# Attention and routing on one core: scores with the directions as weights, routing by groups of four, the current token's products on the vector and activation engines, four matmuls of zeros

## The chip, the core and the metric

The kernel runs on one core of a Trainium2 chip. The core has a tensor engine (PE, with its weight loads shown apart as PEld), a vector engine (DVE), an activation engine (ACT), a general engine (POOL) and a queue engine (SP) that issues most transfers. Each works through its own list of instructions in order and waits for the others by semaphores. The metric is the device time of one execution in microseconds (us); shorter is better.

## The reference, cut to what matters

Three stages follow each other: a linear attention with a decaying state, a mixture of experts that sends each token to the expert with the highest score, and a second mixture with a quota for each expert. The change touches the first stage and the routing for the second.

```
batch, n_heads, seq, head_dim = (4, 8, 768, 48)
for t in range(S):
    cur = np.einsum('bhd,bhe->bhde', u[None] * kt, vt)
    y[:, :, t] = np.einsum('bhd,bhde->bhe', rt, state + cur)
    state = wt[:, :, :, None] * state + np.einsum('bhd,bhe->bhde', kt, vt)
...
en = expert_emb / (np.linalg.norm(expert_emb, axis=-1, keepdims=True) + 1e-06)
logits = xn @ en.T / tau
expert_idx = np.argmax(logits, axis=1)
```

x has 3072 tokens of 384 numbers; there are 8 experts, so 8 directions (the rows of `en`).

## The kernel before, in words

The attention runs over 24 chunks, six of 128 tokens for each of the four batches. A chunk is called a step here. For each step the kernel does the following; lines are those of the kernel before.

- `s2`, on DVE: two scans make the products of decays, forward (`PI`, L283) and backward (`RI`, L291); with them r and k become `rp` (L289) and `kp` (L295). The current token's products are `z` = r times u (four ACT instructions, L298) times k (one POOL instruction on 128x512, L299).
- `s3`: PE turns `kp` into `pT` (ACT copies it to `kT`) and multiplies `kp` by `rp` (`A`, L317); DVE masks that to `am` (two instructions, L321). PE turns `z` (`pz`, L325), DVE sums it for each head to `cs` (L327), and POOL multiplies v by it to `cv` (L329).
- `s4`: PE makes the step's addition to the state (`KV`, L344) and the output `y` from the state before (`Sb`, L347) and from `am` (L350). DVE updates the state (`tm`, `Sc`), ACT copies it to `Sb` (L362), and DVE adds `cv` to `y`: that is `x` (L364), the 128 tokens that the next stage gets.
- `s5`, one step behind: PE turns `x` (`pX`, L375), ACT copies it to `xT` and takes the squares.
- `s6` and `s6b`, the routing: PE multiplies `xT` by the eight directions `enT` (L388); ACT copies the scores to `LG`; DVE finds the maximum, its index and the one-hot row `oh` (L391 to L397); three small matmuls (L398, L399, L401) count the tokens that went to each expert before; DVE picks the row's number from that and turns it into an integer, `di`.
- `s7`: POOL scatters the 128 rows of `x` to the list of their expert (`xg`, L421), two such transfers a step from step 9 on.

Beside this, from step 4 on, pieces of the first experts' weights are split in two parts: ACT rounds a piece to `whi` (L187), and POOL takes the rest, `wlo` (L188, twelve instructions on 128x768). `heat` (L263) puts matmuls of a block of zeros into PE's list, two behind `A` (`HA`) and five behind `y` (`HY`); nothing reads their result. The order on each engine is set by the framework's scheduler. Some of POOL's work (tables for a later stage, `wlo`, scatters) is held back until the next step's `cv` by `issue_after`.

Of the kernel before, what the change touches and what calls it, by code (L numbers as in the profile page):

```python
# [24 lines left out]
NST = B * NC  # L25
# [50 lines left out]
WNQ = 2  # L76
HA = 2
HY = 5
# [3 lines left out]
def tile_kernel(ctx: ExitStack, tc, rd, kd, wd, vd, ud, emb, tau, m1w1, m1w2, m1w2t, wg2, m2w1, m2w2, out):  # L82
# [41 lines left out]
    for t in seeds + Sb:  # L124
# [10 lines left out]
                            channel_multiplier=-1)  # L135

# [98 lines left out]
    with tc.tile_pool(name="ld", bufs=3) as ld, tc.tile_pool(name="wk", bufs=2) as wk, \  # L235
            tc.tile_pool(name="ps", bufs=1, space=PSUM) as ps:

        def route_consts():
# [12 lines left out]
            pE = ps.tile([128, KT, 128], F32, name="pX")  # L251
# [26 lines left out]
        def s2(st):  # L278
# [18 lines left out]
            for p in range(HP):  # L297
                nc.scalar.activation(z[:, p], rr[:, p], AF.Copy, scale=ut[:, p:p + 1])  # L298
            nc.gpsimd.tensor_tensor(z, z, kk, op=ALU.mult)  # L299
            d["PI"] = PI  # L300

        def s3(st):
# [26 lines left out]
            d["cvi"] = nc.gpsimd.tensor_tensor(cv, d["v"], bcast(cs[:, :, None], [128, H, D]), op=ALU.mult)  # L329
# [52 lines left out]
        def s6(st):  # L382
            d = G[st]
            xT = d["xT"]
            yn = G[st + 1]["y"] if st + 1 < NST else ps.tile([128, 512], F32, name="y", bufs=2)
            pG = d["pG"] = yn[:, DM:DM + 2 * E].rearrange("p (a e) -> p a e", a=2)
            for kt in range(KT):
                nc.tensor.matmul(pG[:, 0, :], xT[:, kt, :], enT[:, kt, :], start=(kt == 0), stop=(kt == KT - 1))  # L388
            nc.scalar.copy(LG[:, st, :], pG[:, 0, :])
            mx = wk.tile([128, 8], F32, name="mx")  # L390
            nc.vector.max(mx, LG[:, st, :])  # L391
            mi = wk.tile([128, 8], U32, name="mi")
            nc.vector.max_index(mi, mx, LG[:, st, :])
# [50 lines left out]
        for st in range(NST):  # L444
# [803 lines left out]
```

## Time and profile before

| | us |
|---|---|
| median of 3 runs (852.36 to 856.16) | 855.87 |
| the profiled execution's own time | 852.17 |
| its span, first to last instruction | 850.4 |
| step 0's `x` begins | 24.0 |
| step 23's `x` begins | 225.9 |
| first transposition of the second stage's rows | 243.2 |

The span lies 1.8 us inside the execution's time. The attention takes the first quarter of it; after 243 us the two mixtures follow, which the change leaves as they are.

### The profile page before, as it was taken

How to read it: one execution, taken by the hardware profiler on the slowest of the kernel's cores; microseconds unless marked ns; L12 is line 12 of the kernel's file. 1: busy time of each engine (PE TensorE's matmuls, PEld its weight loads, DVE VectorE, ACT ScalarE, POOL GpSimd, SP SyncE). 2: the span in 40 equal slices, each digit the busy share in tenths (PEclk: the TensorE clock that was granted, in tenths of full speed). 3: DMA queues.
4: the chain of work that ended last, by engine and by line, in shares of the span. 5: the costliest groups of instructions: out<-in, count | busy, mean ns of one | idle time of the engine just before them, and what ended most of it. 6: DMA issues, size and time to landing. Idle time of an engine off the chain costs nothing.

```text
span 850.4 us, 14966 instructions
## 1 busy us (share of the span) xinstructions
PE 776.8 (91%) x5484; PEld 681.1 (80%) x5484; DVE 554.7 (65%) x1740; ACT 319.9 (38%) x763; POOL 227.9 (27%) x220
## 2 busy tenths in 40 slices
PE   5898998999989998999989999697979889899997
PEld 3787787888659897998989787485868778789997
DVE  9688899999534355344543546676878778787430
ACT  3334444443323454344443411423323323235431
POOL 4235477853200303203123002302021210112011
PEclk9799899999989999999999999787969979899999
DMA  8567457661253243433523002422323242426300
GB/s 277 167 193 247 137 185 249 189 202 39 66 181 116 102 149 100 158 114 106 184 88 105 5 1 84 150 87 100 124 72 140 80 154 94 145 69 223 122 29 29
DMA packets 39303, 107.66 MB, mean 127 GB/s; under 512 B 6666, under 2 KB 16700, under 8 KB 39228
## 3 DMA queue, kind: packets, MB, share of 16 engines
q1 hardware_dynamic: 32060, 87.71, 31.5%
q0 software_dynamic: 7168, 18.98, 6.3%
q8 instruction: 44, 0.72, 0.3%
q14 instruction: 31, 0.25, 0.1%
HBM read 87.16 MB, written 19.90 MB: 126 GB/s over the span
## 4 chain that ended last, share of the span: by engine, by line
PE 46%; issue 15%; DVE 4%; POOL 2%; DMA 1%; ACT 1%; another core or an unknown queue 1%; ACTq 0%; POOLq 0%; DVEq 0%
PE pY L520 7%; PE pY L518 7%; PE pY L519 6%; PE pH L518 6%; PE pH L519 6%; PE pH L520 6%; PE pO L657 2%; PE pcm L1081 1%; PE pcn L953 1%; DVE wlo L1120 1%; PE pX L624 1%; POOL x L1094 1%; POOL out_dram L1163 1%; PE pX L1134 1%
## 5 line engine op out<-in xcount | busy, mean ns | idle before, releaser
L515 DVE SCALAR_TENSOR_TENSOR hl<-pH,hh 128x416 fp32r<-128x416 f32 x64 | 37.6, 589 | 66.4 <-ACT hh L514 48.5
L518 PE MATMUL pH<-xhi,whi 128*128 128x416 f32 x192 | 72.1, 376 | 9.5 <-DVE hl L515 7.8
L1120 DVE TENSOR_TENSOR wlo<-stage,whi 128x384 fp32r<-128x384 f32 x128 | 68.3, 549 | 6.9 <-ACT whi L1119 6.8
L518 PE MATMUL pH<-x2h,whi 128*128 128x384 f32 x192 | 71.1, 371 | 1.8 <-DVE h2l L515 1.6
L734 POOL DMA_INDIRECT lg<-lr,ids x24 | 23.0, 959 | 179.6 <-DVE lr L659 173.2
L519 PE MATMUL pH<-x2l,whi 128*128 128x384 f32 x192 | 71.1, 371 | 0.0
L520 PE MATMUL pH<-x2h,wlo 128*128 128x384 f32 x192 | 70.1, 365 | 0.0
L1119 ACT CAST whi<-stage 128x384 fp32r<-128x384 f32 x128 | 57.0, 511 | 32.7 <-PE pH L519 19.3
L520 PE MATMUL pH<-xhi,wlo 128*128 128x416 f32 x192 | 69.0, 359 | 0.0
L519 PE MATMUL pH<-xlo,whi 128*128 128x416 f32 x192 | 68.6, 357 | 0.0
L518 PE MATMUL pY<-whi,h2h 128*128 128x384 f32 x192 | 67.7, 353 | 0.0
L520 PE MATMUL pY<-whi,h2l 128*128 128x384 f32 x192 | 67.7, 355 | 0.0
L1163 POOL DMA_INDIRECT out_dram<-orow,ix x24 | 24.3, 1015 | 159.3 <-ACT orow L1162 144.6
L519 PE MATMUL pY<-wlo,h2h 128*128 128x384 f32 x192 | 66.9, 350 | 0.0
L514 ACT ACTIVATE h2h<-pH 128x384 fp32r<-128x384 f32 x64 | 31.4, 490 | 93.8 <-PE pH L520 92.7
L188 DVE TENSOR_TENSOR wlo<-stage,whi 128x512 fp32r<-128x512 f32 x78 | 48.3, 684 | 24.8 <-ACT whi L187 24.8
L187 ACT CAST whi<-stage 128x512 fp32r<-128x512 f32 (+1 forms) x90 | 51.9, 647 | 31.5 <-PE pY L519 23.0
L520 PE MATMUL pY<-hh,wlo 128*128 128x416 f32 x168 | 60.5, 360 | 0.0
L518 PE MATMUL pY<-hh,whi 128*128 128x416 f32 x168 | 60.1, 359 | 0.0
L519 PE MATMUL pY<-hl,whi 128*128 128x416 f32 x168 | 59.1, 352 | 0.0
L350 PE MATMUL y<-vv,am 128*128 128x48 f32 x384 | 56.9, 273 | 0.0
L1094 POOL DMA_INDIRECT x<-y,ix x24 | 29.8, 1244 | 93.2 <-issue 52.4
(320 smaller groups left out, 1976.2 us busy)
## 6 DMA issues: line engine op xcount, KB each, us to landing
stage<-in_m1w_dram SPq DMA_DIRECT2D x32, 768.0 KB
stage<-in_m2w_dram SPq DMA_DIRECT2D x32, 768.0 KB
wz<-in_w_dram SPq DMA_DIRECT2D x24, 260.0 KB
rd<-in_r_dram SPq DMA_DIRECT2D x24, 256.0 KB
kd<-in_k_dram SPq DMA_DIRECT2D x24, 256.0 KB
xg<-zt SPq DMA_DIRECT2D x8, 627.2 KB
xr<-xg SPq DMA_DIRECT2D x24, 193.0 KB
vv<-in_v_dram SPq DMA_DIRECT2D x24, 192.0 KB
```

Of the source, the lines that this page charges most:

```text
L187: nc.scalar.copy(hi[:, s], t[:, o:o + g])
L188: (eng or nc.vector).tensor_tensor(lo[:, s], t[:, o:o + g], hi[:, s].bitcast(F32), op=ALU.subtract)
L350: yi = nc.tensor.matmul(y[:, o:o + D], ams[h][:, p, :], vv[:, 2 * p + h, :], start=(c == 0), stop=(c == 0 or h == 1))
L514: nc.scalar.activation(hi, pH, AF.Relu)
L515: nc.vector.scalar_tensor_tensor(lo, pH, 0.0, hi.bitcast(F32), op0=ALU.max, op1=ALU.subtract)
L518: nc.tensor.matmul(o, wh, xh, start=start, stop=False)
L519: nc.tensor.matmul(o, wh, xl, start=False, stop=False)
L520: pe[0] = nc.tensor.matmul(o, wl, xh, start=False, stop=stop)
L1094: gi = nc.gpsimd.indirect_dma_start(out=xr[:, a, :], out_offset=None, in_=y1, in_offset=bass.IndirectOffsetOnAxis(ap=ix[:, a:a + 1], axis=0))
L1119: nc.scalar.copy(hi[:, c], t[:, r * g:r * g + g])
L1120: (nc.vector if e == "v" else nc.gpsimd).tensor_tensor(lo[:, c], t[:, r * g:r * g + g], hi[:, c].bitcast(F32), op=ALU.subtract)
L1163: s_ = nc.gpsimd.indirect_dma_start(out=out, out_offset=bass.IndirectOffsetOnAxis(ap=d["ix"][:, a:a + 1], axis=0), in_=orow, in_offset=None)
```

## The change

The scores of a step become a product with the directions as the stationary operand: 8 rows by 128 tokens, written to partitions 32i to 32i+7 of the last quarter of one PSUM tile, `pxl`, whose first three quarters take `pX`. After four steps (the groups are 4, 4, 4, 4, 4, 2, 1, 1) `choose` copies that quarter, turns it once on PE and does the choice for all tokens of the group at once; `place`, a step later, does the counting matmuls for the group. `z` is four DVE instructions with two tensors and u in one. `cv` is eight ACT instructions, one a head. `HY` goes from 5 to 2, so a step has four matmuls of zeros. The `issue_after` is gone.

```
-HY = 5
+HY = 2
...
+        pxl = ps.tile([128, 512], F32, name="pX")
+        nc.vector.memset(pxl, 0.0)
...
             for p in range(HP):
-                nc.scalar.activation(z[:, p], rr[:, p], AF.Copy, scale=ut[:, p:p + 1])
-            nc.gpsimd.tensor_tensor(z, z, kk, op=ALU.mult)
+                nc.vector.scalar_tensor_tensor(z[:, p], rr[:, p], ut[:, p:p + 1], kk[:, p], op0=ALU.mult, op1=ALU.mult)
...
-            d["cvi"] = nc.gpsimd.tensor_tensor(cv, d["v"], bcast(cs[:, :, None], [128, H, D]), op=ALU.mult)
+            for h in range(H):
+                nc.scalar.activation(cv[:, h], d["v"][:, h], AF.Copy, scale=cs[:, h:h + 1])
...
+            i, n = slot_of[st]
+            lgt = pxl[32 * i:32 * i + E, DM:]
             for kt in range(KT):
-                nc.tensor.matmul(pG[:, 0, :], xT[:, kt, :], enT[:, kt, :], start=(kt == 0), stop=(kt == KT - 1))
...
-            nc.tensor.matmul(pG[:, 1, :], tri, oh, start=True, stop=False)
-            nc.tensor.matmul(pG[:, 1, :], ones, base8, start=False, stop=(cum[0] is None))
...
+                nc.tensor.matmul(lgt, enT[:, kt, :], xT[:, kt, :], start=(kt == 0), stop=(kt == KT - 1))
+
+
+        def choose(s0, n, y):
+            lt = wk.tile([128, 128], F32, name="lt", bufs=1)
+            nc.scalar.copy(lt, pxl[:, DM:])
+            nc.tensor.transpose(y[:, DM:], lt, ident)
+            lg = y[:, DM:].rearrange("p (i c) -> p i c", c=32)[:, :n, :E]
+            nc.scalar.copy(LG[:, s0:s0 + n, :], lg)
+            mx = wk.tile([128, GS], F32, name="mx")[:, :n]
+            nc.vector.reduce_max(mx, lg, axis=AX.X)
+            key = wk.tile([128, GS, E], BF16, name="key")[:, :n]
+            nc.vector.tensor_tensor(key, lg, bcast(mx[:, :, None], [128, n, E]), op=ALU.is_equal)
+            nc.vector.tensor_mul(key, key, rev4[:, :n])
+            km = wk.tile([128, GS], F32, name="km")[:, :n]
+            nc.vector.reduce_max(km, key, axis=AX.X)
+            oh = wk.tile([128, GS, E], BF16, name="oh")[:, :n]
+            nc.vector.tensor_tensor(oh, key, bcast(km[:, :, None], [128, n, E]), op=ALU.is_equal)
+            pre = wk.tile([128, GS + 1, E], BF16, name="pre")
+            nc.vector.tensor_copy(pre[:, 0], cum[0])
+            for i in range(n):
+                nc.vector.tensor_add(pre[:, i + 1], pre[:, i], oh[:, i])
+            cum[0] = pre[:, n]
+            return oh, pre[:, :n]
+
+        def place(s0, n, oh, pre, y):
+            pR = y[:, DM:DM + GS * E][:, :n * E]
+            flat = "p i e -> p (i e)"
+            nc.tensor.matmul(pR, tri, oh.rearrange(flat), start=True, stop=False)
+            nc.tensor.matmul(pR, ones, base4[:, :n].rearrange(flat), start=False, stop=False)
+            nc.tensor.matmul(pR, ones, pre.rearrange(flat), start=False, stop=True)
+            sel = wk.tile([128, GS, E], F32, name="sel")[:, :n]
+            nc.vector.tensor_mul(sel, pR.rearrange("p (i e) -> p i e", i=n), oh)
+            de = wk.tile([128, GS], F32, name="de")[:, :n]
+            nc.vector.reduce_sum(de, sel, axis=AX.X)
+            di = wk.tile([128, GS], I32, name="di", bufs=4)
+            nc.vector.tensor_copy(di[:, :n], de)
...
-            if st > 1:
-                s6b(st - 2)
             s4(st)
+            if chosen:
+                place(*chosen.pop(), G[st]["y"])
             if st > 0:
                 s6(st - 1)
-            with tc.issue_after(G[min(st + 1, NST - 1)]["cvi"].ins):
...
+            if st in ends:
+                chosen.append(ends[st] + choose(*ends[st], G[st]["y"]))
```

On DVE, this is the list from the backward scan of step 12 to the state of step 10, in the kernel before (`MAX` and `MAX_INDEX` are the search of the routing, `sel,de` the choice of the row's number):

```order
L291 SCALAR_TENSOR_TENSOR RI<-wz,seed_94 128x516
L395 CAST ef<-mi 128x1
L321 TENSOR_TENSOR am<-A,mask 128x512
L397 TENSOR_SCALAR oh<-io_102,ef 128x8
L295 TENSOR_TENSOR kp<-kd,RI 128x512
L406 TENSOR_TENSOR cum<-oh,cum 128x8
L327 TENSOR_REDUCE cs<-pz 128x8
L414 SCALAR_TENSOR_TENSOR sel,de<-y,oh 128x8
L357 TENSOR_TENSOR tm<-KV,Sc 128x192
L416 CAST di<-de 128x1
L364 TENSOR_TENSOR x<-y,cv 128x384
L359 TENSOR_TENSOR Sc<-tm,PI 128x192
```

The same place in the changed kernel, from the backward scan of step 6 to the state of step 4, ahead of the first choice:

```order
L303 SCALAR_TENSOR_TENSOR RI<-wz,seed_94 128x516
L310 SCALAR_TENSOR_TENSOR z<-rd,ut,kd 128x128
L307 TENSOR_TENSOR kp<-kd,RI 128x512
L310 SCALAR_TENSOR_TENSOR z<-rd,ut,kd 128x128 x2
L332 TENSOR_TENSOR am<-A,mask 128x512 x2
L338 TENSOR_REDUCE cs<-pz 128x8
L369 TENSOR_TENSOR tm<-KV,Sc 128x192
L376 TENSOR_TENSOR x<-y,cv 128x384
L371 TENSOR_TENSOR Sc<-tm,PI 128x192
```

Five of the routing's instructions are gone from between the large ones, three of the step's four `z` stand here instead, and both masks now stand together behind them.

On PE, the end of a step's `y` in the kernel before, with the counting matmuls between the last products (`tri` and `ones` are their weights):

```order
L347 MATMUL y<-Sb_96,rp 128x96
L350 MATMUL y<-vv,am 128x48
L398 LDWEIGHTS tri
L398 MATMUL y<-oh,tri 128x8
L399 LDWEIGHTS ones
L399 MATMUL y<-base_108,ones 128x8
L401 LDWEIGHTS ones
L401 MATMUL y<-cum,ones 128x8
L350 MATMUL y<-vv,am 128x48
L263 LDWEIGHTS ones
```

The same place in the changed kernel:

```order
L359 MATMUL y<-Sb_96,rp 128x96
L362 MATMUL y<-vv,am 128x48 x2
L275 LDWEIGHTS ones
L275 MATMUL KV<-hz,ones 128x320
L275 LDWEIGHTS ones
L275 MATMUL KV<-hz,ones 128x320
L400 MATMUL pX<-xT,enT 8x128 x3
L320 MATMUL pT<-ident,kp 128x128 x4
L328 MATMUL A<-rp,kp 128x128 x8
```

No counting matmul stands inside `y` here, two matmuls of zeros follow it instead of five, and the scores moved from between the `A` products to ahead of them.

On ACT, one step of the kernel before:

```order
L311 COPY kT<-pT 128x512
L365 COPY x<-idf 128x2
L379 ACTIVATE sqb,ss<-x 128x384
L362 COPY Sb_96<-Sc 64x4x48 x2
L389 COPY LG<-y 128x8
L298 ACTIVATE z<-rd,ut 128x128 x2
L377 COPY xT<-pX 128x384
```

One step of the changed kernel:

```order
L322 COPY kT<-pT 128x512
L341 ACTIVATE cv<-vv,cs 128x48 x8
L374 COPY Sb_97<-Sc 64x4x48 x2
L389 COPY xT<-pX 128x384
L391 ACTIVATE sqb,ss<-x 128x384
L377 COPY x<-idf 128x2
```

The eight `cv` stand directly ahead of the copies of the state, which the next step's `y` waits for.

## Rows read from the trace of the kernel before

**Rows 1.** Stretches: busy us by engine, granted clock, transfers' share, GB/s.
```profile
24.00:63.40 39.40, 36.36 (x327) 31.62 (x325) 30.88 (x80) 14.06 (x45) 11.30 (x13) 0.87 0.59 187
63.40:112.70 49.30, 44.42 (x392) 37.24 (x393) 43.14 (x100) 22.16 (x64) 25.05 (x21) 0.87 0.54 179
112.70:174.10 61.40, 56.42 (x557) 48.69 (x557) 60.88 (x139) 28.29 (x87) 47.51 (x35) 0.96 0.71 227
174.10:225.90 51.80, 51.09 (x509) 43.74 (x508) 43.72 (x125) 20.56 (x68) 20.84 (x19) 1.00 0.26 82
225.90:243.20 17.30, 12.81 (x56) 4.33 (x53) 7.41 (x54) 3.94 (x10) 2.91 (x7) 1.00 0.37 118
```

**Rows 2.** The same view, around places where the clock was lower.
```profile
31.60:41.80 10.20, 10.20 (x53) 8.68 (x52) 4.88 (x14) 2.42 (x8) 0.83 (x1) 0.50 0.50 159
69.40:79.40 10.00, 7.24 (x78) 5.75 (x77) 9.96 (x24) 3.05 (x10) 6.55 (x6) 1.00 0.67 232
79.40:82.80 3.40, 3.40 (x19) 2.58 (x20) 2.41 (x8) 0.54 (x2) 0.83 (x1) 0.51 0.46 140
```

**Rows 3.** Timeline, DVE, 197 to 234 us: start, us, instruction.
```profile
197.69 1.23 DVE L283 TENSOR_TENSOR_SCAN PI<-wz,ind 128x516 f32<-128x516 f32 x1
...
205.53 1.23 DVE L283 TENSOR_TENSOR_SCAN PI<-wz,ind 128x516 f32<-128x516 f32 x1
...
207.47 0.16 DVE L391 MAX8 mx<-LG 128x8 f32<-128x8 f32 x1
...
207.63 0.66 DVE L289 TENSOR_TENSOR rp<-rd,PI 128x512 f32<-128x512 f32 x1
...
210.13 0.22 DVE L397 TENSOR_SCALAR oh<-io,ef 128x8 bf16<-128x8 f32 x1
...
230.50 0.17 DVE L391 MAX8 mx<-LG 128x8 f32<-128x8 f32 x1 [1.01 <-ACT LG L389]
...
233.08 0.14 DVE L416 CAST di<-de 128x1 int32<-128x1 f32 x1
```

**Rows 4.** Timeline, POOL and DVE, 148 to 155 us.
```profile
148.12 2.01 POOL L188 TENSOR_TENSOR wlo<-stage,whi 128x768 fp32r<-128x768 f32 x1
148.49 2.73 DVE L283 TENSOR_TENSOR_SCAN PI<-wz,ind 128x516 f32<-128x516 f32 x1
...
153.39 1.49 POOL L299 TENSOR_TENSOR z<-z,kd 128x512 f32<-128x512 f32 x1
...
154.38 0.53 DVE L397 TENSOR_SCALAR oh<-io,ef 128x8 bf16<-128x8 f32 x1
```

**Rows 5.** Groups by line, 20 to 226 us: busy us, mean ns.
```profile
L283 DVE TENSOR_TENSOR_SCAN PI<-wz,ind 128x516 f32<-128x516 f32 x21 | 34.0, 1619 | 0.2
L299 POOL TENSOR_TENSOR z<-z,kd 128x512 f32<-128x512 f32 x22 | 32.9, 1496 | 42.2 <-ACT z L298 23.2 <-ACT x L365 16.7 <-DVE oh L397 2.1
...
L298 ACT ACTIVATE z<-rd,ut 128x128 f32<-128x128 f32 x84 | 28.6, 394 | 20.2 <-PE pz L325 8.8 <-issue 6.4 <-POOL wlo L188 4.9
...
L188 POOL TENSOR_TENSOR wlo<-stage,whi 128x768 fp32r<-128x768 f32 x12 | 24.8, 2070 | 9.3 <-ACT whi L187 9.3
...
L397 DVE TENSOR_SCALAR oh<-io,ef 128x8 bf16<-128x8 f32 x22 | 12.0, 548 | 0.1
...
L365 ACT COPY x<-idf 128x2 f32<-128x2 f32 x23 | 4.4, 190 | 0.1
```

**Rows 6.** Timeline, PE, 205 to 212 us.
```profile
205.38 0.81 PE L388 MATMUL y<-enT,xT 128*128 128x8 f32 x6
206.12 0.72 PE L317 MATMUL A<-rp,kp 64*128 64x128 f32 x8
206.77 0.45 PE L263 MATMUL KV<-hz,ones 128*128 128x320 bf16 x2
...
211.32 0.84 PE L263 MATMUL KV<-hz,ones 128*128 128x320 bf16 x5
```

**Rows 7.** Waits of PE, 20 to 226 us: total us, times, longest.
```profile
PE y L398 <- DVE oh L397: 10.0, 12, 1.6
```

More of the change, by code (lines that the diff above doesn't have):

```diff
@@ L76 @@
 WNQ = 2
+GROUPS = (4, 4, 4, 4, 4, 2, 1, 1)
+GS = max(GROUPS)
 HA = 2
-HY = 5
+HY = 2
 @with_exitstack
@@ new lines, in place @@
+        def place(s0, n, oh, pre, y):
[10 more added lines that the diff above has]
+            nc.vector.tensor_copy(di[:, :n], de)
+            for i in range(n):
+                ready.append((di[:, i:i + 1], G.pop(s0 + i)["x"]))
@@ L419, in s7 @@
         def s7():
             di, x = ready.pop(0)
-            s = nc.gpsimd.indirect_dma_start(out=xg, out_offset=bass.IndirectOffsetOnAxis(ap=di[:, :1], axis=0),
+            s = nc.gpsimd.indirect_dma_start(out=xg, out_offset=bass.IndirectOffsetOnAxis(ap=di, axis=0),
                                              in_=x, in_offset=None)
@@ L443, in tile_kernel @@
         early = (x for i, e in ((0, 0), (1, 0), (0, 1)) for x in wparts(i, e, WNQ, nc.gpsimd))
+        ends, chosen, slot_of = {}, [], {}
+        for n in GROUPS:
+            s0 = len(slot_of)
+            ends[s0 + n] = (s0, n)
+            for i in range(n):
+                slot_of[s0 + i] = (i, n)
         for st in range(NST):
@@ L457, in tile_kernel @@
                 s5(st - 1)
-            if st > 1:
-                s6b(st - 2)
             s4(st)
+            if chosen:
+                place(*chosen.pop(), G[st]["y"])
             if st > 0:
                 s6(st - 1)
-            with tc.issue_after(G[min(st + 1, NST - 1)]["cvi"].ins):
-                for _ in range(TB):
-                    if st > 1 and tables:
-                        table()
-                if st > WST:
-                    next(early, None)
-                if st == WF:
-                    wfold(E - DEF)
-                if st > E:
-                    for _ in range(NSC):
-                        if ready:
-                            s7()
+            if st in ends:
+                chosen.append(ends[st] + choose(*ends[st], G[st]["y"]))
+            for _ in range(TB):
+                if st > 1 and tables:
+                    table()
+            if st > WST:
+                next(early, None)
+            if st == WF:
+                wfold(E - DEF)
+            if st > E:
+                for _ in range(NSC):
+                    if ready:
+                        s7()
         for _ in early:
@@ L479, in tile_kernel @@
         s5(NST - 1)
-        s6b(NST - 2)
+        last_y = ps.tile([128, 512], F32, name="y", bufs=2)
+        place(*chosen.pop(), last_y)
         s6(NST - 1)
-        s6b(NST - 1)
+        end_y = ps.tile([128, 512], F32, name="y", bufs=2)
+        place(*ends[NST], *choose(*ends[NST], last_y), end_y)
         while ready:
```

42 lines of the change are left out of this document (10 added, 32 removed).

## The prediction

> **What bounds the kernel now.** I first cut the attention into stretches of whole steps [rows 1]; the reader is to see which engine is full in each. From 24.0 to 63.4 us (steps 0 to 4) PE works 36.36 of 39.40 us at a granted clock of 0.87. From 63.4 to 112.7 (five steps) PE and DVE both have gaps, 44.42 and 43.14 of 49.30, again at 0.87: a step takes 9.86 us. From 112.7 to 174.1 (seven steps of 8.77) DVE is full, 60.88 of 61.40. From 174.1 to 225.9 (seven steps, no `wlo` any more) PE is full, 51.09 of 51.80, at full clock; a step there takes 7.84 us from one forward scan to the next [rows 3]. So the bound changes hands, and what leaves one engine is worth little where the other is full.
>
> Next, what makes the two slow. DVE: the forward scan needs 1.23 us alone [rows 3], but 2.73 when it starts 0.37 us behind a `wlo` of 2.01 us on POOL; it ends 1.09 us after that one's end, as if it had started there [rows 4]. In the same way the small `oh` takes 0.53 beside POOL's `z` instead of 0.22 [rows 3, 4]. On average the scan takes 1.62 and `oh` 0.55 [rows 5]. PE: its longest sum of waits is for `oh`, 10.0 us in 12 waits, up to 1.6 us [rows 7]. Clock: from 31.6 to 41.8 us it stood at 0.50, the 1.2 GHz level, and from 79.4 to 82.8 at 0.51. In the 10 us ahead of the second fall PE worked only 7.24 us, while DVE was full [rows 2].
>
> **The change part by part.** *z on DVE.* Four instructions a step on 128x128. The trace has none of that form, so I go between two rows: 128x512 (`rp`) lasts 0.66, 128x8 (`mx`) 0.16, and starts lie 0.08 apart for two small ones (207.47 to 207.63 with one between), so about 0.08 of a duration is hidden [rows 3]. In a straight line from 0.08 at 8 to 0.58 at 512 elements, 128 cost 0.20 us; the ends are 0.15 (a quarter of 0.58) and 0.28 (nothing of the duration hidden). I take 0.20, nearest the small row: +0.8 us a step on DVE, 0.6 to 1.1.
>
> *Routing by groups.* Nine small DVE instructions a step go, at 0.08 each 0.72. A group has thirteen, on at most 32 elements; at 0.08 to 0.10 that is 1.2 for four steps, 0.3 a step. Net -0.4.
>
> *Relief from POOL.* `oh` loses its extra 0.33 us a step (0.548 against 0.22) [rows 3, 5]. POOL's 22 `z`, 32.9 us, go altogether, and `cv` with them; the twelve `wlo`, 24.8 us, stay, and keep their scans waiting [rows 5]. In sum DVE has +0.8 -0.4 -0.33: about nothing, +0.1 a step. The four `z` and the two full-width products are now the things that can run into `wlo`; that there is less to run into than before I count at nothing either way (end: 0.3 a step more, if each of the twelve `wlo` costs half a microsecond more).
>
> *PE.* Three matmuls of zeros fewer: (0.84 - 0.45)/3 = 0.13 each, 0.39 a step. The scores took 0.74 from their start to the next product's. They keep three products of two passes, now with 128 columns to move; the nearest row is `A` with 128 columns, 0.65 for eight, 0.081 a pass, so 0.49 (ends: 0.13 x 128/320 a pass, 0.3, and 0.74) [rows 6]. That is -0.25. Counting three times a group instead of a step, plus a transposition, is under -0.1. A full step falls from 7.84 to 7.15 us (6.9 to 7.4), and the waits for `oh` inside `y` disappear, because `place` comes a step later.
>
> The Trainium skill's price is lower: by TensorE: Matmul & The Clock Gate (LDWEIGHTS (loading the stationary operand), Back-to-back issue gap) a load scales with its columns, eight here, and 128 columns cost some 56 ns, so the scores would cost 0.33 and the step 7.0 (an estimate from that page); no row here shows such a load.
>
> *ACT.* Four `z` (0.394 each) go, eight `cv` come; between 0.19 (2 columns) and 0.394 (128 columns) 48 columns cost 0.26, so 2.1 for 1.6 [rows 5]. ACT is busy 28.29 of 61.40 [rows 1], so the sum is free. But the eight stand ahead of `Sb`, and wait for `cs` first. `tm`, `x` and `Sc` follow `cs` on DVE meanwhile, so `Sb` is later than before by what is left of the 2.1 us when `Sc` is done, at most about 1 us by my estimate. What is late next is the first product of the next `y` on PE. Its cover is the 1.5 us by which a step of 8.7 on DVE is longer than PE's 7.15. I count nothing; where PE sets the pace the cover is gone, and it costs up to 1 us a step.
>
> *Start and end.* Before 24 us DVE makes `z` for three steps (2.4 us) in a stretch where it also loses less to POOL: +1.5, between 0 and 2.4. At the end the last token's routing takes 230.50 to 233.08 and its rows leave then [rows 3]; now a 128x128 copy on ACT (0.394, as `z` [rows 5]) and a transposition with its hand-overs come ahead of it: +1.0 (0.4 to 1.5).
>
> **The sum.** Steps 0 to 4: 39.40 = four steps of 7.84, plus 5.1 lost to the half clock over 10.2 us, plus 2.9 of waiting; with 7.5 a step (PE 7.15 and hand-overs), the same clock and 1.4 less waiting, 36.5: -3. Steps 4 to 9: DVE's own 43.14 stays and the waits for `oh` go; PE needs 5 x 7.15 = 35.8 plus the clock's 0.13 x 49.3 = 6.4, so the end is near DVE's sum plus a few waits, 45: -4. Steps 9 to 16: DVE stays full: 61.4 to 60, -1.5, mostly since the `wlo` can now start without POOL's other work ahead of them and so lie earlier. Steps 16 to 23: the last two have no scans and are PE's, -0.6 each; the five before are DVE's at (43.72 - 6.8)/5 = 7.4 (I take 3.4 for each of the last two) against up to 7.84 now, -0.3 each: -2.5. Together -11, start and end +2.5: **-8.5 us**. From the profiled execution's own 852.2 that is 843.7, so **844**. The median of the runs is 3.7 us above that execution, so a median of the changed kernel could come out up to 847 with the same gain.
>
> **The rivals.** *DVE takes it all back (about no change).* If `z` costs 0.28, DVE gets 0.3 more a step, 6.3 us over the 21 steps whose scans lie behind 20 us [rows 5]; the gain shrinks to about 2 and the time is 850. For it: DVE full in 61 us of the attention. Against it: DVE's 128x8 rows at 0.16.
>
> *Slower: the clock falls more often.* DVE holds the pace, PE has 7.15 us of work in a step of 8.7 and three matmuls of zeros fewer, so the long stretch from step 9 on could go as steps 4 to 9 do now, at 0.87 and 9.86 us. That costs 7 x 1.1 = 7.6, from step 16 on 5 x 0.5 = 2.5 more, and steps 0 to 9 gain nothing; with start and end's 2.5 the time is about 865. For it: the fall behind 7.24 us of work in 10 [rows 2]. Against it: the single waits for `oh` are gone, and from 112.7 on PE worked 92% and the clock stood at 0.96. It decides from about seven falls of 3.4 us more than now, each worth half its length.
>
> *The clock stays up.* Then the 5.1 us of the first stretch and the 6.4 of the second come back too, as far as DVE lets them: -4 and -3 more, and 837. The row's fall came behind waits of 1.6 us at most [rows 2, 7], so shorter waits alone need not keep it up. The Trainium skill (TensorE: Matmul & The Clock Gate, HAM oscillation — how this bites in real kernels) has long idle gaps between bursts lower the clock; by that rule none is left here and this would be the result, but the rows do not bear it out.
>
> **How the numbers follow.** The forecast, 839 to 848: 0.52. No change: 0.20. Clock stays up, or DVE freed more than thought, 828 to 839: 0.15. Slower: 0.13. The range 834 to 858 leaves out about a third of the gain's far side and half of the slow side, some 2 in 10. The likeliest case alone has 839 to 848. A measurement of this kernel tells about 0.5% (4.3 us) from no change. Faster by more: the forecast and the clock case, with a little lost at the near end, 0.66; within: 0.21; slower by more: 0.13.
>
> **What would show it.** PE's step at the end near 7.2 us, waits of PE for `oh` gone, and in their place waits for `am` or `x` on DVE. DVE still over 95% from 112 to 165 us, with `z` near 0.28 as a duration and scans of 2.7 beside `wlo`. Scores near 0.5 us a step. The attention's last `x` near 216 instead of 225.9, and about 18 us from there to the second stage's first transposition. Wrong if `z` lasts over 0.35, if PE waits for `Sb`, or if rows of clock 0.5 appear after 113 us.

## The result, and the profile after

The changed kernel took 844.6 us in the median of 4 runs (840.2 to 846.3), the kernel before 855.6 beside it (852.4 to 856.2): a ratio of 0.989, with a 95% interval of 0.985 to 0.993. So it is faster by about 1.1%, and the forecast of 844 and its likeliest case came out. The profiled execution of the changed kernel, however, was the slowest of its four (846.3 us, span 844.4), and lies only 5.9 us below the profiled one of before. The traces below answer for those 5.9 us, the runs for 11. The medians and ranges given here are of all runs of a kernel; a run more than 1.5% above its kernel's fastest is left out of the ratios and of the differences between kernels.

The first view cuts the attention at the same steps as [rows 1]: 0 to 4, 4 to 9, 9 to 16, 16 to 23, and from the last `x` to the second stage. Columns: stretch and length, busy time of PE, PE's weight loads, DVE, ACT and POOL with the number of instructions, granted clock, DMA share, GB/s.

```profile
23.20:55.50 32.30, 30.59 (x306) 25.73 (x306) 31.97 (x62) 17.64 (x62) 3.82 (x2) 1.00 0.76 241
55.50:110.60 55.10, 46.93 (x361) 39.57 (x361) 49.95 (x95) 27.17 (x86) 22.99 (x13) 0.75 0.61 202
110.60:166.40 55.80, 53.95 (x519) 45.78 (x516) 53.25 (x122) 29.41 (x106) 10.26 (x9) 0.97 0.61 190
166.40:216.30 49.90, 49.43 (x473) 40.57 (x471) 42.92 (x117) 28.53 (x107) 8.10 (x8) 1.00 0.30 97
216.30:234.40 18.10, 12.50 (x57) 4.38 (x56) 8.02 (x56) 3.79 (x11) 4.86 (x9) 0.97 0.30 100
```

Against before the four stretches moved by -7.1, +5.8, -5.6 and -1.9 us, the tail by +0.8. So one stretch lost, and the others gained more than it. The second and the third belong together: DVE is busy 6.8 us more in steps 4 to 9 and 7.6 less in 9 to 16, since nine of the twelve pieces (a piece is one `whi` and its `wlo`) now lie in the first of the two and one in the second. In steps 4 to 9 DVE and PE have gaps besides (49.95 and 46.93 of 55.10), and the clock was granted at 0.75 where before it had 0.87.

Most of the first stretch's 7.1 us is clock: it held 1.00 here, and before it stood at 0.50 from 31.6 to 41.8 us [rows 2], which cost the 5.1 us that the prediction names. Just ahead of that fall PE had waited, until 29.81 us, for the directions to be made ready. It is the longest of PE's waits between 20 and 226 us in that trace, and the changed kernel's list, below, has none for them:

```profile
PE pX L253 <- DVE am L250: 2.3, 1, 2.3
```

But this gain is not steady. In another execution of the changed kernel (after_again, below) the clock fell at about 16 us, though PE had waited up to there no longer than here (6.3 and 2.1 us against 6.1 and 2.1, before the first products), and steps 0 to 4 took 39.7 us:

```profile
24.80:64.50 39.70, 39.70 (x304) 33.22 (x303) 29.14 (x62) 17.61 (x61) 2.15 (x2) 0.73 0.58 183
```

With the start (0.8 earlier) the attention and its tail give 8.8 us; the 610.0 us behind the second stage's first transposition were 607.2 before, which the change does not touch.

What happens in steps 4 to 9 is in the timeline around 68 us (start, duration, engine, line, operation; in brackets idle time and what ended it):

```profile
66.97 1.55 ACT L195 CAST whi<-stage 128x768 fp32r<-128x768 f32 x2
...
67.86 3.73 POOL L196 TENSOR_TENSOR wlo<-stage,whi 128x768 fp32r<-128x768 f32 x2 [14.38 <-ACT whi L195]
68.03 3.97 DVE L310 SCALAR_TENSOR_TENSOR z<-rd,ut,kd 128x128 f32<-128x128 f32 x3
...
71.92 1.28 DVE L332 TENSOR_TENSOR am<-A,mask 128x512 f32<-128x512 f32 x2
...
72.75 1.57 PE L328 MATMUL A<-rp,kp 64*128 64x128 f32 x9 [2.64 <-DVE am L332]
```

ACT casts two pieces in a row, POOL takes their `wlo` back to back, and three `z` on DVE, which alone need 0.33 each, last 3.97 together. `am` and the `A` behind it are late by that, PE stands for 2.64 us, and then the clock falls:

```profile
72.90:86.60 13.70, 13.70 (x77) 11.47 (x77) 9.90 (x21) 3.68 (x14) 4.54 (x4) 0.50 0.55 190
100.30:114.00 13.70, 9.46 (x49) 7.74 (x49) 11.75 (x24) 4.90 (x13) 5.88 (x3) 0.51 0.46 148
```

Before, the attention had one fall of 10.2 us and five of 3.4 ([rows 2] shows the first two), 27.2 us in all. Here there are one of 3.4, at 55.9 us, and these two of 13.7, together 30.8. The second begins amid seven `wlo` that POOL takes from 91.8 us on; a wait of PE of 4.24 us ahead of `A` lies inside it and so did not start it.

PE's sums of waits, to be held against [rows 7]:

```profile
PE A L328 <- DVE am L332: 4.4, 2, 2.6
PE A L328 <- DVE oh L417: 4.2, 1, 4.2
PE y L359 <- ACT Sb L374: 3.2, 3, 1.5
PE y L428 <- DVE oh L417: 1.0, 1, 1.0
```

The twelve waits for `oh` inside `y` have gone but for one. Two for `am` (2.64 and 1.71 us) took their place, with a third of 4.24 us (named `oh` ahead of `A`, it is the same kind: the list of DVE was late behind three `wlo`).

A step with no piece in it, on DVE, for [rows 3]:

```profile
181.57 0.55 DVE L376 TENSOR_TENSOR x<-y,cv 128x384 f32<-128x384 f32 x1
182.03 1.22 DVE L295 TENSOR_TENSOR_SCAN PI<-wz,ind 128x516 f32<-128x516 f32 x1
183.17 0.33 DVE L310 SCALAR_TENSOR_TENSOR z<-rd,ut,kd 128x128 f32<-128x128 f32 x1
...
186.07 0.61 DVE L310 SCALAR_TENSOR_TENSOR z<-rd,ut,kd 128x128 f32<-128x128 f32 x2
186.60 1.28 DVE L332 TENSOR_TENSOR am<-A,mask 128x512 f32<-128x512 f32 x2
...
188.52 0.55 DVE L376 TENSOR_TENSOR x<-y,cv 128x384 f32<-128x384 f32 x1
```

From `x` to `x` it takes 6.95 us, and no routing stands in it. (Taken from scan to scan, as 7.84 was before, the steps here take 7.26 to 7.49, in the mean 7.35.) Two `z` take 0.61, from start to the next start 0.53, so one costs 0.27.

PE in the same step, for [rows 6]:

```profile
186.70 0.43 PE L275 MATMUL KV<-hz,ones 128*128 128x320 bf16 x2
187.07 0.82 PE L400 MATMUL pX<-xT,enT 128*8 128x128 f32 x6
187.82 0.66 PE L320 MATMUL pT<-ident,kp 128*128 128x128 f32 x4
```

The scores take 0.75 to the next product's start, as before; the two matmuls of zeros 0.37.

The groups from 20 to 226 us, for [rows 5] (busy, mean ns, then idle time ahead):

```profile
L341 ACT ACTIVATE cv<-vv,cs 128x48 f32<-128x48 f32 x184 | 44.0, 322 | 22.7 <-DVE cs L338 22.1 <-DVE am L332 0.5
L310 DVE SCALAR_TENSOR_TENSOR z<-rd,ut,kd 128x128 f32<-128x128 f32 x86 | 38.8, 462 | 0.0
L295 DVE TENSOR_TENSOR_SCAN PI<-wz,ind 128x516 f32<-128x516 f32 x21 | 27.3, 1301 | 0.3 <-DVE sel L432 0.3
...
L196 POOL TENSOR_TENSOR wlo<-stage,whi 128x768 fp32r<-128x768 f32 x12 | 23.4, 1969 | 71.9 <-ACT whi L195 71.9
```

The scans lost most of their lengthening (1.30 for 1.62), and `z` took it over: 0.46 in the mean against 0.33 undisturbed. The Trainium skill (SBUF — State Buffer, Who interferes with whom) says that a VectorE operation with two inputs in SBUF and a GpSimd operation that reads SBUF shut each other out for a whole instruction. The trace agrees: `z` began 0.17 us behind the `wlo` and ended 0.4 us after the pair had.

### The profile page after: what moved, and what is told of

It reads as the page before. It is cut to its first block, busy times and chain, and to the rows that moved or that the text cites. A ratio compares the mean times of both kernels' runs of the same rounds, so it can differ in the third digit from the quotient of the medians.

```text
span 844.4 us, 14670 instructions
## 1 busy us (share of the span) xinstructions
PE 771.9 (91%) x5373; PEld 675.0 (80%) x5373; DVE 556.1 (66%) x1719; ACT 335.5 (40%) x851; POOL 168.0 (20%) x173
## 4 chain that ended last, share of the span: by engine, by line
PE 53%; issue 9%; DVE 4%; POOL 2%; another core or an unknown queue 1%; ACT 1%; DMA 1%; ACTq 0%; POOLq 0%; DVEq 0%
PE pH L548 8%; PE pY L550 7%; PE pY L548 7%; PE pH L549 7%; PE pH L550 7%; PE pY L549 7%; PE pO L687 2%; PE pX L654 2%; PE pcm L1111 1%; PE pcn L983 1%; DVE wlo L1150 1%; POOL x L1124 1%; POOL out_dram L1193 1%; PE pX L1164 1%
## 5 line engine op out<-in xcount | busy, mean ns | idle before, releaser
L548 PE MATMUL pH<-xhi,whi 128*128 128x416 f32 x192 | 73.8, 385 | 11.7 <-DVE hl L545 7.5
L544 ACT ACTIVATE h2h<-pH 128x384 fp32r<-128x384 f32 x64 | 31.4, 491 | 91.8 <-PE pH L550 90.8
L764 POOL DMA_INDIRECT lg<-lr,ids x24 | 23.1, 961 | 185.9 <-DVE lr L689 180.7
L544 ACT ACTIVATE hh<-pH 128x416 fp32r<-128x416 f32 x64 | 32.8, 515 | 62.5 <-PE pH L550 48.5
```

The costliest lines, as they stand in the source:

```text
L544: nc.scalar.activation(hi, pH, AF.Relu)
L548: nc.tensor.matmul(o, wh, xh, start=start, stop=False)
L764: s = nc.gpsimd.indirect_dma_start(out=dst, out_offset=bass.IndirectOffsetOnAxis(ap=d["ids"][:m, a:a + 1], axis=0), in_=src, in_offset=Non ...
```

## The experiments

Three sets ran, each on one chip, with the kernel before beside it. That kernel took 861.5, 838.4 and 859.8 us on the three, so kernels are compared within a set. The changed kernel itself ran in the second set alone. Two theories stood after the result. The first: the lists of DVE and PE became shorter, and steps 4 to 9 gave part of it back, since without `issue_after` the pieces come in bunches. The second: the clock falls because the matmuls of zeros are gone. That the new form of the scores saves PE's time was a third matter.

This table has the lengths of the stretches from `x` to `x` of each profiled execution, in us, with the granted clock of two of them; the rows that matter follow below. Each line is one execution, and the same kernel differs between executions: `changed` and `after_again` are one kernel, and so are `pace`, `pace_again` and `pace_base`.

| kernel (set) | steps 0-4 | 4-9 | 9-16 | 16-23 | sum | clock 0-4 | clock 4-9 |
|---|---|---|---|---|---|---|---|
| changed (result) | 32.3 | 55.1 | 55.8 | 49.9 | 193.1 | 1.00 | 0.75 |
| pace (1) | 29.1 | 45.6 | 63.7 | 51.9 | 190.3 | 1.00 | 1.00 |
| zeros5 (1) | 29.9 | 52.2 | 56.1 | 54.4 | 192.6 | 1.00 | 0.91 |
| tokens_as_weights (1) | 32.2 | 51.3 | 53.9 | 50.3 | 187.7 | 1.00 | 0.80 |
| after_again (2) | 39.7 | 51.5 | 55.7 | 49.9 | 196.8 | 0.73 | 0.92 |
| pace_again (2) | 29.0 | 45.7 | 62.0 | 49.8 | 186.5 | 1.00 | 0.96 |
| routing_by_step (2) | 35.4 | 54.7 | 57.0 | 52.4 | 199.5 | 1.00 | 0.78 |
| z_two_engines (2) | 30.0 | 42.4 | 63.5 | 50.0 | 185.9 | 1.00 | 0.96 |
| pace_base (3) | 29.1 | 45.6 | 62.1 | 50.4 | 187.2 | 1.00 | 1.00 |
| pace_vector (3) | 29.0 | 42.3 | 57.5 | 50.5 | 179.3 | 1.00 | 1.00 |
| pace_z (3) | 34.1 | 42.1 | 61.0 | 52.4 | 189.6 | 0.90 | 0.96 |
| pace_zeros5 (3) | 30.5 | 46.3 | 62.5 | 53.3 | 192.6 | 1.00 | 1.00 |

### The pieces spread over the steps

```
-                nc.scalar.activation(cv[:, h], d["v"][:, h], AF.Copy, scale=cs[:, h:h + 1])
+                d["cvi"] = nc.scalar.activation(cv[:, h], d["v"][:, h], AF.Copy, scale=cs[:, h:h + 1])
...
-                next(early, None)
+                with tc.issue_after(G[min(st + 1, NST - 1)]["cvi"].ins):
+                    next(early, None)
```

> The changed kernel, with one edit: the rounding of a weight piece on ACT is put behind the eight cv of its own step, so that one piece a step reaches POOL instead of two or three together. Theory one (bunched pieces): in steps 3 to 9 the gain is given back because POOL runs two or three wlo back to back, DVE's z waits for all of them, PE waits 1.7 to 4.2 us for am, and the clock falls to half for 30.8 us in all between 55 and 114 us. Then single pieces leave waits of at most 1.5 us, less than 14 us of half clock in the attention, and the time goes from 844.6 to 835 to 840. Theory two (zeros): the clock falls because three matmuls of zeros a step are gone; then spreading the pieces changes little, 843 to 846, with 25 us or more of half clock.

Measured: 843.5 us (842.2 to 853.4, 6 runs), a ratio of 0.984 (0.977 to 0.991) to before. The 835 to 840 that the first theory expected were missed (at this ratio 842 on the chip of the result); the half clock of the profiled attention was 13.7 us, in one fall, under the 14 of that theory, and its waits went up to 1.8 us where it had 1.5. Beside no run of the changed kernel the ratio could not be told from 0.989, so it was run again next to it:

> The pieces of weights spread over the steps again, beside the changed kernel on the same chip. The first theory (the bunches of pieces cost what steps 4 to 9 lost) expects 3 to 6 us under the changed kernel, since steps 4 to 9 took 55.1 us there and 45.6 us here in the earlier trace, less what steps 9 to 16 then pay for the pieces that came early (64 against 56 us). If a piece costs the same wherever it stands, the two are within 2 us. The second theory (the matmuls of zeros had held the clock) expects falls of the clock between 55 and 110 us here too.

> The changed kernel once more, as the measure for the three runs beside it on the same chip. Both theories expect a ratio of 0.985 to 0.992 to the kernel before and the same picture in the trace: wlo on GpSimd in bunches of two and three, two or three falls of the clock between 55 and 115 us.

Measured in that set: spread 823.7 (820.4 to 824.7, 5 runs), 0.982 (0.976 to 0.987); changed 829.3 (823.9 to 835.2, 11 runs), 0.990 (0.987 to 0.993). The spread pieces are 5.7 us faster in the medians; the intervals just touch. The clock granted over the whole execution was higher in each of the five runs with spread pieces (0.949 to 0.957) than in any of the eleven of the changed kernel (0.929 to 0.948). Where in the attention the 5.7 us lie, the two traces do not show: in steps 4 to 16 they take 107.2 us (changed) and 107.7, and their whole difference lies in steps 0 to 4, which the clock of after_again made long before the first piece. A third time (label pace_base) it was 844.0 us against 859.8 for before:

> The pieces spread over the steps, as the measure for the three runs beside it on the same chip: a ratio of 0.979 to 0.985 to the kernel before.

Its ratio of 0.986 (0.976 to 0.997) is a little above what was expected, within its interval. Its stretches:

```profile
23.60:52.70 29.10, 29.10 (x293) 24.51 (x291) 28.84 (x62) 15.42 (x58) 0.00 (x0) 1.00 0.73 239
52.70:98.30 45.60, 39.42 (x378) 33.33 (x377) 45.04 (x97) 24.60 (x83) 16.49 (x9) 1.00 0.77 240
98.30:160.40 62.10, 54.17 (x519) 45.54 (x518) 62.07 (x121) 33.59 (x113) 26.08 (x15) 1.00 0.54 173
160.40:210.80 50.40, 49.07 (x465) 40.13 (x461) 42.79 (x116) 28.10 (x106) 8.58 (x8) 1.00 0.33 108
```

With two matmuls of zeros behind `y` the clock stays at 1.00 through all 23 steps of this execution, and DVE is full from step 4 to 16. In the other two it fell once, for 13.7 us, and twice, for 3.4 each, and the clock of steps 4 to 9 was 1.00 and 0.96, where the changed kernel had 0.75 and 0.92. So few zeros alone do not take the clock away in this kernel; in these traces, and by the clocks of all runs of the second set, it falls more where the pieces lie in bunches. A single piece still costs what one of a bunch does, as the timeline at 83 us shows:

```profile
83.35 2.56 POOL L196 TENSOR_TENSOR wlo<-stage,whi 128x768 fp32r<-128x768 f32 x1 [5.57 <-ACT whi L195]
84.23 1.83 DVE L310 SCALAR_TENSOR_TENSOR z<-rd,ut,kd 128x128 f32<-128x128 f32 x1
85.98 0.68 DVE L307 TENSOR_TENSOR kp<-kd,RI 128x512 f32<-128x512 f32 x1
```

The `z` takes 1.75 us to the next start, 1.5 more than its 0.25 to 0.27 alone; in the bunch at 68 us it was 3.89 for three, 1.5 to 1.6 more for each of the two `wlo`. The DVE time lost to a piece is equal in these two places, so steps 9 to 16 are longer here (they now hold seven pieces instead of one) and steps 4 to 9 shorter. That what a bunch adds is PE's longer wait and the clock behind it fits the granted clocks, but it is argued: no single trace shows the 5.7 us.

### Five matmuls of zeros

```
-HY = 2
+HY = 5
```

> The changed kernel with five matmuls of zeros behind y instead of two. Theory one (bunched pieces): PE pays 0.39 us more in steps where it sets the pace, and the clock still falls in steps 3 to 9, over 20 us of half clock: 846 to 851. Theory two (zeros): the half clock between 55 and 114 us drops from 30.8 us to under 14 and the time to 836 to 842.

Measured: 849.5 us (845.3 to 863.6, 10 runs), 0.989 (0.985 to 0.993) to before: the same ratio as the changed kernel's. Each theory got one half right here. The half clock of the profiled attention fell to 13.6 us, under the 14 that the second theory asked for, and steps 4 to 9 have a clock of 0.91 for 0.75; but the 836 to 842 us that it expected did not come, and steps 16 to 23, where PE sets the pace, are 4.5 us longer than in the result's trace. In a kernel with bunches the zeros seem to give back about what they cost; the changed kernel did not run in this set, so that is read from the ratios alone. With the pieces spread it is another matter:

> As the spread pieces, with five matmuls of zeros a step instead of two. If PE sets the pace of the steps without a piece, 0.39 us a step comes back there (some eleven steps: 3 to 5 us more, up to 9 if every step pays). If the zeros lie in PE's waits and hold the clock, within 2 us, and no falls of the clock before 220 us.

Measured: 849.3 us (847.0 to 860.4, 10 runs) against 844.0 for pace_base beside it, 4.4 us more (ratios to before 0.991, 0.987 to 0.995, and 0.986, 0.976 to 0.997: by the intervals alone not told apart, but nine runs at 847.0 to 853.2 all lie above three at 843.3 to 844.0). The two profiled executions are 8.0 us apart, 5.4 of them between the sums of the stretches:

```profile
23.60:54.10 30.50, 30.50 (x306) 25.66 (x305) 28.98 (x61) 15.37 (x58) 0.00 (x0) 1.00 0.75 236
54.10:100.40 46.30, 42.25 (x400) 35.36 (x398) 44.94 (x96) 24.95 (x84) 15.74 (x9) 1.00 0.75 238
100.40:162.90 62.50, 59.99 (x540) 50.14 (x540) 59.37 (x120) 33.20 (x113) 23.64 (x15) 0.92 0.54 172
162.90:216.20 53.30, 51.21 (x484) 41.74 (x482) 43.26 (x117) 28.13 (x106) 8.58 (x8) 1.00 0.31 103
```

Of the 5.4, 1.4 are paid in steps 0 to 4 and 2.9 in 16 to 23, where no piece lies and PE is full; in the twelve steps between, which DVE paces, only 1.1. The clock gained nothing (0.92 in steps 9 to 16, and 0.941 to 0.953 over the nine whole executions, 0.939 to 0.952 over the three of pace_base). With the pieces spread the second theory is out.

The reverse, the kernel before with two instead of five:

```
-HY = 5
+HY = 2
```

> The kernel before with two matmuls of zeros behind y instead of five, alone. By theory one the zeros are only work: PE saves 0.39 us in the steps where it sets the pace (about eleven), -2 to -5 us, and the half clock of the attention stays near 24 to 27 us: 850 to 853. By theory two the clock falls more often: more than 35 us of half clock, 857 or more.

Measured: 856.0 us (848.3 to 870.2, 10 runs) against 861.5, a ratio of 0.992 (0.987 to 0.997), some 7 us. So alone, without the rest of the change, fewer zeros made the kernel before faster. But here the second theory had the clock right: the seven runs that the ratio counts were granted 0.908 to 0.927 over the whole execution, the kernel before beside them 0.925 to 0.942. Fewer zeros lowered the clock in that kernel, and it was faster in spite of it. The profiled execution took 864.0 us, and no row of it is read.

### The tokens as weights, as before

```
-            lgt = pxl[32 * i:32 * i + E, DM:]
+            lgt = pxl[:, DM + 32 * i:DM + 32 * i + E]
...
-                nc.tensor.matmul(lgt, enT[:, kt, :], xT[:, kt, :], start=(kt == 0), stop=(kt == KT - 1))
+                nc.tensor.matmul(lgt, xT[:, kt, :], enT[:, kt, :], start=(kt == 0), stop=(kt == KT - 1))
...
-            lt = wk.tile([128, 128], F32, name="lt", bufs=1)
-            nc.scalar.copy(lt, pxl[:, DM:])
-            nc.tensor.transpose(y[:, DM:], lt, ident)
-            lg = y[:, DM:].rearrange("p (i c) -> p i c", c=32)[:, :n, :E]
+            lg = pxl[:, DM:].rearrange("p (i c) -> p i c", c=32)[:, :n, :E]
```

> The changed kernel with the scores' operands put back: the tokens are the weights, and a step's scores lie at columns 32i to 32i+7 for all 128 tokens, so that the copy lt and its transposition go; the choice by groups stays. If the directions as weights cost PE the same (0.75 us for six passes in the changed kernel's trace, 0.74 before), the time stays or falls by up to 2 us, 842 to 845, most of it at the last token's routing (0.6 to 1 us). If they save PE 0.25 us a step, as I had put it, the time rises by 2 to 5 us, to 847 to 850.

Measured: 849.5 us (845.4 to 852.7, 4 runs), 0.989 (0.981 to 0.997). The scores in PE's timeline:

```profile
181.49 0.73 PE L400 MATMUL pX<-enT,xT 128*128 128x8 f32 x6
182.07 0.64 PE L320 MATMUL pT<-ident,kp 128*128 128x128 f32 x4
```

Six passes with eight columns to move and a full load each take 0.58 to the next start; the changed kernel's six, with eight columns to load and 128 to move, 0.75. The new form is the dearer one by 0.17 a step in this place. The old form took 0.74 in the kernel before, where products of `A` came next [rows 6], so its price hangs on its place in the list. The ratio is that of the changed kernel, as the first reading had it; that 849.5 lies in the range of the second is this chip, on which the kernel before took 861.5.

### Routing by step

```
-GROUPS = (4, 4, 4, 4, 4, 2, 1, 1)
+GROUPS = (1,) * 24
```

> Routing in groups of one step instead of four; all else as changed. If the lists on VectorE set the pace, about 0.4 us a step comes back (thirteen small instructions at 0.08 us a step instead of a quarter of them, less what four choices cost in one), and PE waits for the one-hot again where it stands behind a choice: 6 to 12 us more than the changed kernel. If the time of the routing was beside the path, 0 to 2 us.

Measured: 838.3 us (832.4 to 856.3, 11 runs), 0.999 (0.995 to 1.003) to before, and 8.4 us above the changed kernel beside it. All else of the change is in this kernel, and it is as slow as the kernel before. One step on DVE:

```profile
186.41 0.54 DVE L376 TENSOR_TENSOR x<-y,cv 128x384 f32<-128x384 f32 x1
...
190.81 0.16 DVE L412 TENSOR_TENSOR key<-y,mx 128x8 bf16<-128x8 f32 x1
190.88 0.34 DVE L310 SCALAR_TENSOR_TENSOR z<-rd,ut,kd 128x128 f32<-128x128 f32 x1
191.14 0.15 DVE L413 TENSOR_TENSOR key<-key,rev 128x8 bf16<-128x8 bf16 x1
191.22 0.34 DVE L310 SCALAR_TENSOR_TENSOR z<-rd,ut,kd 128x128 f32<-128x128 f32 x1
...
194.15 0.55 DVE L376 TENSOR_TENSOR x<-y,cv 128x384 f32<-128x384 f32 x1
```

Ten small instructions lie between the large ones, most 0.07 to 0.08 us from their start to the next; the step takes 7.74 from `x` to `x`, the changed kernel's step without routing 6.95. Three steps in a row from scan to scan, with the columns of [rows 1], in the kernel before, this one and the changed one:

```profile
181.64:205.53 23.89, 23.39 (x251) 20.55 (x247) 23.15 (x61) 10.88 (x37) 12.10 (x11) 1.00 0.31 91
171.80:195.70 23.90, 23.06 (x222) 18.98 (x220) 23.32 (x74) 13.13 (x51) 4.04 (x3) 1.00 0.43 129
174.77:196.81 22.04, 21.99 (x226) 18.59 (x226) 22.04 (x50) 11.90 (x43) 4.26 (x4) 1.00 0.32 101
```

By step, a step takes what it took before, 7.97 us; by groups it takes 7.35. DVE is busy 0.43 less a step and PE 0.36 less, because PE too turns the scores and counts in every step here. Both are nearly full, and which of the two savings was needed is not separated by a run. The waits of PE for `oh` are not back, since `place` still comes a step later: PE's largest sum of waits is 10.7 us in 8, for `am`. So the end of the waits that [rows 7] names did not by itself make this kernel faster than the one before.

### The current token's products on two engines

```
-                nc.vector.scalar_tensor_tensor(z[:, p], rr[:, p], ut[:, p:p + 1], kk[:, p], op0=ALU.mult, op1=ALU.mult)
+                nc.scalar.activation(z[:, p], rr[:, p], AF.Copy, scale=ut[:, p:p + 1])
+            nc.gpsimd.tensor_tensor(z, z, kk, op=ALU.mult)
```

> The products of the current token back on ScalarE (four activations) and GpSimd (one multiplication of 128x512); all else as changed. VectorE loses 1.07 us a step of z, but its scans meet GpSimd's multiplication again and take up to 2.7 instead of 1.2 us. The theory that VectorE's list paces the steps, and that the move was worth nothing by itself (1.07 paid, about 0.33 to 1.4 of slowed scans saved), expects within 4 us of the changed kernel, with no bunches of three pieces on GpSimd since its list is longer. If moving z off GpSimd was where the gain came from, 6 to 10 us more than the changed kernel.

Measured: 825.3 us (824.3 to 831.5, 5 runs), 0.988 (0.981 to 0.994), 4.0 below the changed kernel in the medians; by the intervals the two are not told apart. POOL's instructions now lie between the pieces, and most `wlo` stand alone or in pairs with a gap. With the pieces spread:

> As the spread pieces, with the products of the current token on ScalarE and GpSimd as before the change. With the pieces in bunches this was about 4 us less than the changed kernel. If that came from GpSimd's list (with z in it, the pieces could not stand back to back), nothing of it is left here: 0 to 8 us more than the spread pieces, as VectorE meets GpSimd's multiplication in every step. If moving z to VectorE was a loss in itself (1.07 us a step paid for 0.1 to 0.7 us of slowed scans), about 4 us less.

Measured: 846.4 (845.4 to 846.7, 4 runs) against 844.0 for pace_base, 0.989 (0.981 to 0.997). What was gained with the bunches is not gained again, which fits the first reading, that it came from the order of POOL's list. With the pieces spread, `z` on DVE is 2.5 us faster in the medians, and the four runs lie above the three of pace_base; the intervals do not tell the two apart.

### The pieces' second half on DVE

```
-        early = (x for i, e in ((0, 0), (1, 0), (0, 1)) for x in wparts(i, e, WNQ, nc.gpsimd))
+        early = (x for i, e in ((0, 0), (1, 0), (0, 1)) for x in wparts(i, e, WNQ, nc.vector))
```

(on top of the spread pieces)

> As the spread pieces, with each wlo (128x768) computed on VectorE in its own list instead of on GpSimd. On GpSimd a wlo took 1.8 to 2.6 us in the earlier trace, held one of VectorE's instructions (a z of 1.82 in place of 0.33) and lengthened a step from 7.2 to 8.5 to 9.9. On VectorE the later wlo of 128x512 take 0.69 each, so an estimate for one of 128x768 is 1.0. If what a piece costs is VectorE held by GpSimd, the twelve steps with a piece become 0.5 to 1.0 us shorter each: 6 to 12 us less than the spread pieces. If the cost of a piece lies elsewhere (the cast on ScalarE, the transfer of the weights), or VectorE now waits for the cast, the time is the same or up to 5 us more.

Measured: 836.0 us (833.9 to 836.8, 5 runs), a ratio of 0.977 (0.970 to 0.984) to before, 7.9 below pace_base. This is the fastest kernel of the study. At 82 us:

```profile
82.06 0.94 DVE L196 TENSOR_TENSOR wlo<-stage,whi 128x768 fp32r<-128x768 f32 x1
82.91 0.70 DVE L307 TENSOR_TENSOR kp<-kd,RI 128x512 f32<-128x512 f32 x1
```

A `wlo` on DVE takes 0.85 to the next start. On POOL it took 2.56 and held DVE for 1.5. The difference of some 0.65, twelve times, is 7.8, close to what was measured. The groups from 52 to 168 us tell the same, first with `wlo` on POOL:

```profile
L310 DVE SCALAR_TENSOR_TENSOR z<-rd,ut,kd 128x128 f32<-128x128 f32 x52 | 27.8, 546 | 0.0
```

and then with it on DVE:

```profile
L310 DVE SCALAR_TENSOR_TENSOR z<-rd,ut,kd 128x128 f32<-128x128 f32 x56 | 18.2, 346 | 0.0
...
L196 DVE TENSOR_TENSOR wlo<-stage,whi 128x768 fp32r<-128x768 f32 x12 | 11.4, 952 | 0.0
```

`z` falls from 0.55 to 0.35 us in the mean, so DVE takes twelve instructions more and is done sooner. The stretches shrink by 3.3 and 4.6 us, together 7.9.

## Why the prediction was right, point by point

The number was right and so was the sign; the way to it was right in one large term and wrong in several that cancelled. For steps 0 to 4, 4 to 9, 9 to 16, 16 to 23, the start and the end the forecast was -3, -4, -1.5, -2.5, +1.5 and +1.0; the trace has -7.1, +5.8, -5.6, -1.9, -0.8 and +0.8. The sums, -8.5 and -8.8, agree by luck: steps 4 to 9 missed by 9.8 us, and the first, the third and the start missed by 4.1, 4.1 and 2.3 the other way. That the traced execution then lies only 5.9 us below the one before, and the medians 11.0, is not in the forecast either.

- **Routing by groups** (net -0.4 us a step, set off against the dearer `z`). Undoing the grouping costs 8.4 us, nearly the whole 9.1 to before, and the 0.4 a step on DVE came out as 0.43. The prediction had about 0.4 x 21 = 8.4 in DVE's sum, and then thought it eaten by `z`. It put PE's share at under 0.1 a step; the three steps above have 0.36, and the two are not told apart.
- **`z` on DVE** (0.20, ends 0.15 and 0.28). It costs 0.27, the upper end, so +1.07 a step instead of +0.8. The rival "DVE takes it all back" hung on just this price of 0.28, and yet did not come: that the price came true and the gain still came shows that this price alone did not decide. DVE's busy sum over the four stretches was 178.1 us after and 178.6 before, about nothing, as forecast, while the stretches themselves shrank from 201.9 to 193.1. Steps 16 to 23 take 49.9 us with `z` on DVE and 50.0 without it (z_two_engines), for PE is full there (49.43 and 49.12).
- **Relief from POOL** (`oh` loses 0.33; scans keep waiting beside `wlo`). `oh` and the scans did lose most of their lengthening (1.62 to 1.30), but `z` took it over (0.46 in the mean, 0.33 alone). The end I left open, that the four `z` run into `wlo`, is what happened; the sum had it at nothing.
- **"The `wlo` can now start without POOL's other work ahead of them and so lie earlier", -1.5 for steps 9 to 16.** This is the step that failed. They lie earlier, steps 9 to 16 did gain 5.6, but nine of the twelve fell into steps 4 to 9 and two of them before, in bunches of two and three, and steps 4 to 9 lost 5.8 where -4 was forecast. Most of that is work of DVE moved from the one stretch to the other. The removal of `issue_after` is in the diff, and I priced only its good side. Putting it back for the pieces was worth 5.7 us in the medians of one set; that the bunches cost this by the clock is argued.
- **"The same clock" in steps 0 to 4.** This failed too: the half clock of 10.2 us was not there in the traced execution, so the rival "the clock stays up" came true for this stretch and not for the next (0.75). The prediction looked at waits of 1.6 us [rows 7] and left out the one of 2.3 ahead of the first fall. In after_again the stretch fell to 0.73, so this gain hangs on the execution.
- **PE's zeros** (0.13 each, -0.39 a step). Confirmed: 0.77 to 0.37 from the first to the next product for five (zeros5) and two. They are worth 4.4 us with the pieces spread and some 7 in the kernel before, and nothing that can be told in the changed kernel, where the zeros may hold clock that the bunches cost. The slower rival's mechanism, clock falls with fewer zeros, is seen in the granted clocks of before_zeros2, without its loss; it needed seven falls of 3.4 us more than before, and there were 30.8 us of half clock in the attention against 27.2, one more.
- **Scores** (0.74 to 0.49, ends 0.3 and 0.74). No saving: 0.75, the upper end. The mis-sized term is 0.25 a step on PE. No row among those shown ahead has a load of eight columns, but the trace of before does, in a product with 512 columns to move:

```profile
234.09 5.32 PE L211 MATMUL pH<-stage,IW 128*8 128x512 f32 x12 [0.68 <-DVE g L226]
```

  One lasts 0.59, so twelve in 5.32 start 0.43 apart; in a straight line that is 0.11 for 128 columns and 0.65 for the six passes, nearer to what came than the row of `A`. The price from the Trainium skill (TensorE: Matmul & The Clock Gate, Back-to-back issue gap), which gave 0.33 for the scores, is further off: here six passes of fp32 with 128 columns took 0.125 each, and the measurement decides.
- **PE's step at the end** (7.15): 7.35 from scan to scan, as the 7.84 was taken, so 0.5 less where 0.69 was forecast; the 0.25 of the scores is about what is missing. The stretch gained 1.9 against 2.5.
- **ACT**. Eight `cv` take 1.91 us (0.23 from start to start, 0.32 as a duration) for the 2.1 forecast; PE does wait for `Sb` behind them, 3.2 us in three waits in the whole attention, so the cover that I named was there but for those.
- **Start and end** (+1.5 and +1.0): the first `x` came 0.8 earlier, not later, and the tail is 18.1 us against 17.3, +0.8. The last `x` stands at 216.3, as forecast.
- **The signs of being wrong.** Two of the three came: PE waited for `Sb`, and a fall of the clock that began at 100.3 us lasted to 114.0, past 113. `z` lasts 0.33 alone, under 0.35, but 0.46 in the mean, because of `wlo`.

Taken together: grouping -8.4, fewer zeros -4.4, which the bunches (+5.7) took back. That is -7.1, where 11.0 and 9.1 us were measured in two sets. It adds differences of kernels that are not independent, and is only a check. What the move of `z` is worth by itself (2.5 us in favour with the pieces spread, 4.0 against with the bunches, both within the intervals of no change) is not settled, and that of `cv` was not tried.

## What to carry to other kernels

Removing an ordering constraint has two prices, that the work comes earlier and that it comes in a bunch; look where the freed work will lie, and on which engine's operands it then stands. Count small instructions on the engines that are full: taking most of the routing's out of each step was worth 8.4 us here, the largest part of the change that was undone by itself. Compare the clock over all runs before you read a gain out of one trace: the first stretch of one kernel took 32.3 us in one execution and 39.7 in another. And before moving work to an idle engine, ask what it holds while it works: a subtraction of 128x768 cost the full DVE 0.85 us when it did it itself, and 1.5 when POOL did it.

## What the runs showed of the hardware

- An fp32 product with eight columns loaded and 128 to move took 0.125 us a pass; with 128 loaded and eight to move 0.097 in one place of the list (tokens_as_weights) and 0.123 in another (before). The lighter load did not make the pass cheaper.
- `z` of 128x128 with two tensors and a column in one instruction: 0.33 as a duration, 0.27 from start to start on DVE. A 128x48 product on ACT with a column as scale: 0.32 and 0.23.
- The clock fell to 0.50 behind waits of PE of 2.64, 2.3 (before) and 1.71 us; but it stood at 1.00 for the 187 us of 23 steps in which waits went up to 1.8 (pace_base) and PE worked 86% of steps 4 to 9. And two executions of the changed kernel with the same waits up to 16 us went on at 1.00 (steps 0 to 4 in 32.3 us) and at 0.50 (39.7). The length of a single wait does not tell it; what does is left open.
- Even a small instruction pays where two engines meet: `di`, four columns, took 1.71 us beside a `wlo` on POOL (twice in pace_base) and 0.17 without one.
